# First stage of a fused transformer layer: when the weight pieces for the scales are loaded, when the next heads' weights are split, and when GpSimd clears the stacked operands

## The chip, the core and the metric

The kernel runs on one core of a Trainium2 chip. The metric is the time of one execution on the device in microseconds, as the median of several runs. Lower is better.

## What is computed

The reference is a transformer layer whose attention and MLP branch both read the same layer-normalized input, and whose outputs are added to it (2048 rows, 512 columns, 32 heads of 16, MLP width 1792, all float32):

```
xn = _layernorm(x, axis=-1)
return x + _A_ref(xn, A_wqkv, A_wo) + _B_ref(xn, B_w1, B_b1, B_w2, B_b2)

# _A_ref: scores = einsum("bhqd,bhkd->bhqk", q, k) * (Dh ** -0.5); p = softmax(scores)
#         o = einsum("bhqk,bhkd->bhqd", p, v); return o @ wo
# _B_ref: h = gelu(einsum("bsd,df->bsf", x, w1) + b1); return einsum("bsf,fd->bsd", h, w2) + b2
```

## The kernel before

Matrix products run on TensorE in float16, each operand being split into a high and a low half, so that three products (high by high, high by low, low by high) stand for one. Weights are first divided by a power of two near a bound of their size, the scale, which is found from the sum of the absolute values of each row, one weight piece (128x1024 numbers, 512 KB) at a time. ScalarE reads a piece and gives the sum (`total`, line 937, the only use of the piece at that point); the same weights are read again later, when they are split.

Attention is done in units. A task is one group of four heads by one block of 512 queries; it has 16 units, and there are 32 tasks, 512 units. For each unit TensorE computes scores once for their maxima (`pS`, line 174 by way of `s_mm`), of which VectorE takes the row maxima (line 403), and, 19 units later (LEAD), the same scores with the maximum already subtracted (`pT`), of which ScalarE takes the exponential (line 444, four for each unit), and then the product with V (`pV`). Between these, TensorE works on what is dense (`pD`): projections, and later the MLP and the output projection. The maxima of a task are turned into two rows of the stacked operand `qst` by way of a small store to memory and two loads (lines 358 and 363).

The first stage, up to the first exponential, is written as a list of steps (class `Plan`): each step has an engine, an estimated duration, the steps that it comes after, buffers that it takes and frees, and a weight called tail. The planner repeatedly takes the engine that can start first and emits the step with the largest tail among those that can start. It so fixes the order of instructions on every engine. The engines' queues are worked through in that order on the chip; a step waits there for the data and the buffers that it really needs, not for all that the list names. The first stage normalizes x, turns it (`xt`), projects the first heads' Q and K, stacks them by way of memory (`qk_d`, then `kst` and `qst`, line 549), computes V for the first 12 of 16 tiles (`wvh`, copied into `vv` at line 1187), takes the maxima of 19 units, and meanwhile sums 18 weight pieces (line 1249). A piece takes one of three buffers `wch`; its load is issued by SyncE at line 929. When the estimate of its size reaches BULK (600), the planner holds the load back until the transfers ahead of it are nearly done (line 245).

GpSimd clears the stacked operands `kst` and `qst`, two sets of four blocks (line 95; eight fills for each set), and writes V's column of ones (lines 1136 and 1137). These steps wait for nothing in the list before, and have a low tail.

After the first stage the units run. `rest` yields the remaining dense work: four tiles of V, one projection of the first heads, then the projections of the heads m = 1, 2, 3. The weights of the heads m are loaded by `load_qk` (line 606, on SyncE, as a job in a lane that holds back large transfers) and split by `split_qk`: ScalarE makes the high half (line 154), GpSimd the low one (lines 156 and 157). `split_qk` is stepped once for each unit and yields as long as the pair (m, w) is not in `here`:

```
            while (m, w) not in here:
                yield
            split_pool(wh[:, w, 0], wh[:, w, 1], wf[w], inv[:, 8 + 2 * min(m, 2) + w:9 + 2 * min(m, 2) + w])
```

Of the kernel before, what the change touches and what calls it, by code (L numbers as in the profile page):

```python
# [28 lines left out]
NQB = S // QB  # L29
# [10 lines left out]
NV = 12  # L40
PAIRED = (0, 1), (2, 3), (4, 5), ((0, 1), (0, 2)), (6, 7), (8, 9), (10, 11)
SPLIT, SWITCH, SAME, KLAG = 4, 160, 1500, (0, 0, 12000, 12000)
LAG, E_TAIL = 3000, 8000
LANE = 225
WFROM, WSTEP, XN = 10, 4.5, 4.5
VT = 2600, -8000
# [12 lines left out]
def layer_kernel(ctx: ExitStack, tc: tile.TileContext, x, wqkv, wo, w1, b1, w2, b2, out):  # L59
# [30 lines left out]
    def clear(i, blocks=range(NQB), which=(1, 0)):  # L90
        for b in blocks:
            for st, v in ((qst, 0.0), (kst, MROWS)):
                if (st is kst) not in which:
                    continue
                nc.gpsimd.memset(st[i][b].rearrange("p h n -> p (h n)").bitcast(F32), v)
# [57 lines left out]
    def split_pool(hi, lo, src, inv):  # L153
        nc.scalar.activation(hi, src, AF.Copy, scale=inv)
        given("act", 1000)
        nc.gpsimd.tensor_scalar(src, src, inv, 0.0, op0=ALU.mult, op1=ALU.add)
        nc.gpsimd.tensor_tensor(lo, src, hi, op=ALU.subtract)
# [62 lines left out]
    class Plan:  # L220
# [7 lines left out]
        def add(self, engine, ns, fn, after=(), take=(), free=(), size=0, tail=0, gap=0, small=False, lag=0):  # L228
            t = dict(gap=gap, small=small, lag=lag, e=engine, ns=ns, fn=fn, after=[a for a in after if a], take=take, free=free, size=size, tail=tail,
                     end=None, n=len(self.todo))  # L230
            for key in free:
                self.users.setdefault(key, []).append(t)
            self.todo.append(t)
            return t
# [62 lines left out]
    queue, slot = [], [0]  # L297
# [3 lines left out]
    def later(n, fn, local=False, bulk=0):  # L301
        queue.append((slot[0] + n, fn, local, bulk))
# [292 lines left out]
            if self.key is not None:  # L595
                free_banks[self.key[1]].append(self.key[0])

    here = {(1, 0), (1, 1)}

    def load_qk(m):  # L600
        wf = []
        for w in range(2):
            wf.append(ph.tile([P, D], F32, name="wq", bufs=2).rearrange("p (c n) -> p c n", n=P))

            def load(w=w):
                nc.sync.dma_start(wf[w], wqkv[:, w * D + m * P:w * D + (m + 1) * P].rearrange("(c p) n -> p c n", p=P))
                here.add((m, w))

            later(0, load, True, 256)
        return wf  # L610

    def split_qk(m, wf, inv, ready_w):
        wh = ph.tile([P, 2, 2, NC, P], F16, name="wqk_h", bufs=2)
        for w in (1, 0):
            while (m, w) not in here:
                yield
            split_pool(wh[:, w, 0], wh[:, w, 1], wf[w], inv[:, 8 + 2 * min(m, 2) + w:9 + 2 * min(m, 2) + w])
            yield
        ready_w[m] = wh
        if m < 3:  # L620
            later(4, lambda: wfs.append(load_qk(m + 1)), True)
# [229 lines left out]
    with ExitStack() as st1:  # L851
# [44 lines left out]
        add = plan.add  # L896
# [7 lines left out]
        def raw(key, tag, shape, bufs):  # L904
            tl[key] = (px if tag == "xs" else work if tag == "pe" else ph).tile(shape, F32, name=tag, bufs=bufs)
            return tl[key]
# [19 lines left out]
        def piece_in(key, src, after=(), tail=0):  # L926
            def fn():
                tl[key] = raw(key, "wch", [P, 4 * W], 3).rearrange("p (a b) -> p a b", b=src.shape[2])
                nc.sync.dma_start(tl[key], src)
            return add("SP", 420, fn, after, take=[key], size=520 if tail else 700, tail=tail)  # L930

        def total(ns, key, dst, after, done=()):

            def fn():
                v = tl[key]
                o = v if done else junk[:, :v.shape[1] * v.shape[2]].rearrange("p (a b) -> p a b", b=v.shape[2])
                nc.scalar.activation(o, v, AF.Abs, scale=1.0 / SPREAD, accum_out=dst)
            return add("ACT", ns, fn, after if isinstance(after, list) else [after], free=done)
# [34 lines left out]
        q_in = {w: wq_in(0, w) for w in (1, 0)}  # L973
        wvv = wqkv[:, 2 * D:3 * D].rearrange("(c p) n -> p c n", p=P)
        v_in = [piece_in(("wch", "v", i), wvv[:, :, i * W:(i + 1) * W], tail=280000) for i in range(2)]
        x_in += [tile_in(t) for t in range(4, NT)]

# [134 lines left out]
        s_of, s_prev, m_prev = {}, [None], []  # L1112
# [19 lines left out]
        cleared = {}  # L1132
        his, los, w_ready, k_ready, q_ready, t_last, staged = {}, {}, {}, {}, {}, {}, {}
# [3 lines left out]
            nc.gpsimd.memset(vv[:, :, H * VW:], 0.0)  # L1137

        his[0], los[0] = turned(0, normal(0))
        for b in range(NQB):  # L1140
            for w in (1, 0):
                cleared[w, b] = add("POOL", 480, lambda w=w, b=b: clear(0, [b], [w]), tail=-8000)
        cleared["v"] = add("POOL", 1300, clear_v, tail=-8000)
        q_sum = [total(560, ("wq", 0, w), amq[:, w:w + 1], q_in[w]) for w in (1, 0)]
        chain, inv0, fac0 = scale_chain(amq, 2, q_sum, "q0")
        for w in (1, 0):
            wf, hi, lo, i1 = ("wq", 0, w), wqh[:, w, 0], wqh[:, w, 1], inv0[:, w:w + 1]
            h = add("ACT", 620, lambda wf=wf, hi=hi, i1=i1: nc.scalar.activation(hi, tl[wf], AF.Copy, scale=i1), [chain], free=[wf] if w else [])
            if w:
                w_ready[w] = add("DVE", 700, lambda wf=wf, hi=hi, lo=lo, i1=i1: nc.vector.scalar_tensor_tensor(  # L1150
                    lo, tl[wf], i1, hi, op0=ALU.mult, op1=ALU.subtract), [h], free=[wf])
            else:
                a = add("POOL", 800, lambda wf=wf, i1=i1: nc.gpsimd.tensor_scalar(tl[wf], tl[wf], i1, 0.0, op0=ALU.mult, op1=ALU.add), [h])
                w_ready[w] = add("POOL", 1100, lambda wf=wf, hi=hi, lo=lo: nc.gpsimd.tensor_tensor(lo, tl[wf], hi, op=ALU.subtract), [a], free=[wf])
        a = add("DVE", 90, lambda: nc.vector.tensor_tensor(sexp[:, 0:1], fac0[:, 0:1], fac0[:, 1:2], op=ALU.mult), [chain])
        a = add("DVE", 90, lambda: nc.vector.tensor_scalar_mul(sexp[:, 0:1], sexp[:, 0:1], DH ** -0.5), [a])
        add("ACT", 800, lambda: fetch_scale(0), [a])
# [8 lines left out]
        for i in range(2):  # L1166
            hi, lo = (wvh[j][:, :, i * W:(i + 1) * W] for j in range(2))
            key = ("wch", "v", i)
# [4 lines left out]
            else:  # L1173
                b = add("POOL", 1240, lambda key=key: nc.gpsimd.tensor_scalar(
                    tl[key], tl[key], inv_v[:, 0:1], 0.0, op0=ALU.mult, op1=ALU.add), [h])
# [62 lines left out]
        def low(t):  # L1238
            t["tail"] = -20000
# [6 lines left out]
        for n, src in enumerate(every[:NM]):  # L1246
            key = ("wch", "m", n)
            dst = am_all[:, 12 + n:13 + n] if n < 2 else am_all[:, n - 2:n - 1] if n < 9 else amx[:, n - 2:n - 1]
            low(total(1150, key, dst, piece_in(key, src, k_ready[1]), done=[key]))

        def fill(a, b):
            if b - a > 500 and not s_of:
# [338 lines left out]
```

## Time and profile before

| What | Value |
|---|---|
| Time, median of 3 runs | 1469.04 us (1466.7 to 1472.21) |
| Time of the profiled execution | 1471.15 us |
| Its span, first to last instruction | 1469.4 us |
| TensorE busy | 1440.3 us (98%) |
| VectorE busy | 1348.5 us (92%) |
| ScalarE busy | 1257.0 us (86%) |
| GpSimd busy | 689.4 us (47%) |
| Granted TensorE clock, mean | 0.992 |

The profile is one execution. A row of the order of time gives the start and the duration in us, the engine, the line, the operation, what it writes and reads, how many in a row, and, in brackets, how long the engine was idle ahead of it and what ended that. PE is TensorE, PEld its weight loads, DVE VectorE, ACT ScalarE, POOL GpSimd, SPq the DMA queue that SyncE issues to. A window gives the busy time and the count of each engine in a stretch, the granted TensorE clock as a share of full speed, the busy share of the 16 DMA engines and what they moved in GB/s. "Issue" is time in which an engine waited for nothing that the profile shows.

### The profile page before, as it was taken

The numbers are of one execution on the slowest core, as the hardware profiler recorded it, in microseconds if no ns is written. First come the engines' busy times: TensorE is split into PE (matmuls) and PEld (weight loads), VectorE is DVE, ScalarE is ACT, GpSimd is POOL, SyncE is SP. The second block draws the span as 40 slices with busy tenths as digits, with TensorE's granted clock in tenths as the row PEclk, the third lists the DMA queues.
The fourth block names the chain that finished last, engine by engine and source line by source line (L and its number), as shares of the span: only waits on it lengthen the run. The fifth ranks groups of instructions, "written<-read, shape, count | busy, mean of one in ns | idle before, by whom it ended". The sixth has DMA issues, their size and how long they took to land.

```text
span 1469.4 us, 90770 instructions
## 1 busy us (share of the span) xinstructions
PE 1440.3 (98%) x41229; PEld 974.2 (66%) x41229; DVE 1348.5 (92%) x2236; ACT 1257.0 (86%) x2394; POOL 689.4 (47%) x774
## 2 busy tenths in 40 slices
PE   8979999999999999999999999999999999999998
PEld 4546667766666777766677766666666667666664
DVE  7869799999999999999999999999999999999933
ACT  6548788888999988899988899998889998888885
POOL 5101665755778521268941137783126787212200
PEclk9999999999999999999999999999999999999999
DMA  6550455546323311131112111122102110212413
GB/s 204 179 178 4 152 156 181 164 146 211 107 62 95 100 45 33 38 87 44 52 36 78 42 44 41 44 87 59 38 16 87 58 37 20 59 54 78 118 58 109
DMA packets 111482, 124.98 MB, mean 85 GB/s; under 512 B 21244, under 2 KB 83068, under 8 KB 111096
## 3 DMA queue, kind: packets, MB, share of 16 engines
q1 hardware_dynamic: 111096, 119.18, 26.5%
q8 instruction: 322, 5.28, 1.5%
q14 instruction: 64, 0.52, 0.1%
HBM read 81.66 MB, written 37.34 MB: 81 GB/s over the span
## 4 chain that ended last, share of the span: by engine, by line
PE 90%; DVE 4%; DMA 2%; ACT 1%; issue 1%; SPq 1%; POOL 0%; POOLq 0%; DVEq 0%; ACTq 0%
PE pD L174 27%; PE pV L174 26%; PE pT L174 21%; PE pS L174 16%; DVE mt L403 3%; DMA wq<-in_A_wqkv_dram 1%; PE pT L1049 0%; PE pD L1049 0%; DMA wch<-in_A_wo_dram 0%; ACT pe L444 0%; DMA rb<-den_d 0%; DMA den_d<-dn 0%; DVE wvh L1171 0%; DMA ot_d<-ot 0%; ACT pe L1002 0%
## 5 line engine op out<-in xcount | busy, mean ns | idle before, releaser
L403 DVE TENSOR_REDUCE mt<-pS 128x1 f32<-128x512 f32 x2029 | 1279.6, 684 | 55.6 <-PE pS L174 19.5
L444 ACT ACTIVATE pe<-pT 128x512 f32<-128x512 f32 x2048 | 1109.1, 599 | 150.2 <-PE pT L174 66.6
L174 PE MATMUL pV<-pe,vv 64*32 64x512 f32 x8192 | 1090.4, 592 | 0.3
L174 PE MATMUL pT<-qst,kst 64*32 64x512 f16 x8192 | 707.7, 379 | 7.9 <-ACT pe L444 7.8
L174 PE MATMUL pS<-kst,qst 62*32 62x512 f16 x8116 | 630.8, 379 | 1.9 <-issue 1.8
L174 PEld LDWEIGHTS <-qst 62*32 62x32 f16 x8192 | 312.0, 91 | 184.9 <-issue 36.2
L174 PE MATMUL pD<-xb,wc 64*32 64x512 f16 x5376 | 363.1, 375 | 0.0
L174 PE MATMUL pD<-w_s,g 64*32 64x512 f16 x5376 | 361.5, 375 | 0.0
L174 PEld LDWEIGHTS <-kst 64*32 64x32 f16 x8192 | 279.6, 91 | 106.3 <-issue 35.3
L174 PEld LDWEIGHTS pV<-pe,vv 64*32 64x32 f32 x8192 | 241.8, 106 | 14.0 <-PE pV L174 5.8
L174 PEld LDWEIGHTS <-wc 64*32 64x32 f16 x5376 | 160.4, 91 | 45.0
L174 PEld LDWEIGHTS <-g 64*32 64x32 f16 x5376 | 162.7, 91 | 39.1 <-issue 0.3
L174 PE MATMUL pD<-xt,wqk_h 64*32 64x512 f16 x2400 | 161.9, 379 | 1.4 <-issue 1.4
L371 POOL TENSOR_SCALAR mparts<-mx 128x16 f16<-128x16 f32 x32 | 6.6, 206 | 303.0 <-DVE mx L369 303.0
L1433 POOL TENSOR_TENSOR xa<-xa,yt 128x512 f32<-128x512 f32 x16 | 20.5, 1282 | 166.2 <-ACT yt L1431 166.1
L174 PEld LDWEIGHTS <-wqk_h 64*32 64x32 f16 x2592 | 78.6, 93 | 25.0 <-issue 6.2
L1387 POOL TENSOR_TENSOR t<-t,hh 128x512 f32<-128x512 f32 x56 | 71.9, 1284 | 4.7
L1380 POOL TENSOR_TENSOR t<-t,hh 128x512 f32<-128x512 f32 x56 | 71.8, 1283 | 4.5
L1385 POOL TENSOR_TENSOR t<-hh 128x512 f32<-128x512 f32 x56 | 58.3, 1042 | 21.7 <-ACT hh L1408 19.3
L1382 POOL TENSOR_TENSOR g<-t,g 128x512 f16<-128x512 f32 x56 | 65.3, 1165 | 4.7
L501 POOL TENSOR_TENSOR osb<-osb,rb 128x512 f32<-128x512 f32 x31 | 39.9, 1287 | 49.7 <-ACT pe L444 31.9
L174 PE MATMUL pD<-wo_s,oc 64*32 64x512 f16 x816 | 55.0, 376 | 0.0
(161 smaller groups left out, 968.0 us busy)
## 6 DMA issues: line engine op xcount, KB each, us to landing
wc<-w_d SPq DMA_DIRECT2D x56, 256.0 KB
qk_d<-stg SPq DMA_DIRECT2D x32, 256.0 KB
rb<-den_d SPq DMA_DIRECT2D x124, 64.0 KB
wch<-in_B_w_dram SPq DMA_DIRECT2D x14, 512.0 KB
wch<-in_B_w_dram SPq DMA_DIRECT2D x28, 256.0 KB
w_d<-wsp SPq DMA_DIRECT2D x28, 256.0 KB
kst<-qk_d SPq DMA_DIRECT2D x64, 96.0 KB
qst<-qk_d SPq DMA_DIRECT2D x64, 96.0 KB
```

The lines of the kernel that those rows point to most:

```text
L174: p = nc.tensor.matmul(*args, **kw)
L371: lambda: nc.gpsimd.tensor_scalar(parts[:, :, 0], mx[:, 0], 1.0 / MROW, 0.0, op0=ALU.mult, op1=ALU.add),
L403: nc.vector.reduce_max(mt_of[t][:, n // 2 + n % 2 * 2, qt, kb:kb + 1], s, axis=AX.X)
L444: nc.scalar.activation(pe, st, AF.Exp, scale=scale_of[g // 2])
L501: pooled((1280, lambda: nc.gpsimd.tensor_tensor(osb, osb, rb, op=ALU.mult)), (620, lambda: nc.gpsimd.tensor_scalar(ot[:, 0], osb, 1.0, 0.0 ...
L1380: (1280, lambda: nc.gpsimd.tensor_tensor(t1, t1, hh, op=ALU.mult)),
L1382: (1160, lambda: nc.gpsimd.tensor_tensor(g[:, 1, f, :], t1, g[:, 0, f, :], op=ALU.subtract)),
L1385: pooled((1040, lambda: nc.gpsimd.tensor_tensor(t1, hh, hh, op=ALU.mult)), (620, lambda: nc.gpsimd.tensor_scalar(t1, t1, 1.0, 1.0 / GELU_A ...
L1387: (1280, lambda: nc.gpsimd.tensor_tensor(t1, t1, hh, op=ALU.mult)),
L1433: add = lambda: nc.gpsimd.tensor_tensor(xa, xa, yt, op=ALU.add)
```

## The change

Four edits. The load of piece n in the first stage comes, in the planner's list, after the maximum number 3 n instead of after K's second block is stacked, and its size is estimated at 610 instead of 700 (still above BULK). `here` now holds the unit from which a split may come, four later than the one in which the load was issued. The clears of the first set and V's ones come after K's weights are split (`w_ready[1]`); those of the second set still wait for nothing.

```
-LAG, E_TAIL = 3000, 8000
+LAG, E_TAIL, MSTEP = 3000, 8000, 3.0
...
-    here = {(1, 0), (1, 1)}
+    here = {(1, 0): 0, (1, 1): 0}
...
-                here.add((m, w))
+                here[m, w] = slot[0] + 4
...
-            while (m, w) not in here:
+            while here.get((m, w), 1 << 30) > slot[0]:
                 yield
...
-            return add("SP", 420, fn, after, take=[key], size=520 if tail else 700, tail=tail)
+            return add("SP", 420, fn, after, take=[key], size=520 if tail else 610, tail=tail)
...
-        for b in range(NQB):
-            for w in (1, 0):
-                cleared[w, b] = add("POOL", 480, lambda w=w, b=b: clear(0, [b], [w]), tail=-8000)
-        cleared["v"] = add("POOL", 1300, clear_v, tail=-8000)
...
+        for b in range(NQB):
+            for w in (1, 0):
+                cleared[w, b] = add("POOL", 480, lambda w=w, b=b: clear(0, [b], [w]), [w_ready[1]], tail=-8000)
+        cleared["v"] = add("POOL", 1300, clear_v, [w_ready[1]], tail=-8000)
...
-            low(total(1150, key, dst, piece_in(key, src, k_ready[1]), done=[key]))
+            low(total(1150, key, dst, piece_in(key, src, [m_prev[int(MSTEP * n)]]), done=[key]))
```

What this does to the order of instructions. ScalarE at the end of the first stage, before: L937 is the sum of a piece, L1187 the copy of a tile of V, L382 the copy of the first task's maxima, L444 the exponential.

```order
L382 ACTIVATE mturned<-pS 64x64
L937 ACTIVATE wch,amx<-wch 128x1024 x2
L1187 ACTIVATE vv<-pD 128x32x16
L1187 ACTIVATE vv<-pT 128x32x16
L937 ACTIVATE wch,amx<-wch 128x1024
L1187 ACTIVATE vv<-pT 128x32x16 x2
L937 ACTIVATE wch,amx<-wch 128x1024 x4
L444 ACTIVATE pe<-pT 128x512 x14
```

The same place after the change:

```order
L937 ACTIVATE wch,amx<-wch 128x1024 x2
L382 ACTIVATE mturned<-pS 64x64
L937 ACTIVATE wch,amx<-wch 128x1024 x3
L1187 ACTIVATE vv<-pD 128x32x16
L1187 ACTIVATE vv<-pT 128x32x16 x3
L444 ACTIVATE pe<-pT 128x512 x14
```

The four sums that stood between the last copy of V and the first exponential are gone from there; the last three sums now stand ahead of the last four copies of V.

ScalarE in the units, where the weights of the heads m = 2 are split (L154; L470 and L656 are copies of a finished V product and a finished projection), as a piece of the difference:

```order
 L470 ACTIVATE osb<-pV 128x512
-L444 ACTIVATE pe<-pT 128x512 x2
-L154 ACTIVATE wqk_h<-wq,inv_2910 128x512
-L444 ACTIVATE pe<-pT 128x512 x2
-L656 ACTIVATE pf<-pD 128x512
-L444 ACTIVATE pe<-pT 128x512 x2
-L154 ACTIVATE wqk_h<-wq,inv_2910 128x512
+L444 ACTIVATE pe<-pT 128x512 x4
+L656 ACTIVATE pf<-pD 128x512
 L444 ACTIVATE pe<-pT 128x512 x10
```

The first split stood two exponentials behind the copy L470; it now stands behind fourteen, twelve later, and the second one four behind it as before. The splits of m = 1 and m = 3 are where they were, counted in exponentials, and from the MLP on TensorE's order is the same as before.

SyncE in the first stage, a piece of the difference from the store of the keys' last block on: L929 is the load of a piece, L1106 and L1105 the stores of a projection's halves, L549 the load of a stacked operand.

```order
 L549 DMA kst_1_80<-qk_d 48x2x512 x2
-L929 DMA wch<-in_A_wqkv_dram 128x4x256 x2
-L929 DMA wch<-in_B_w_dram 128x4x256
+L929 DMA wch<-in_B_w_dram 128x4x256 x5
 L1106 DMA qk_d<-stg 128x512
 L1105 DMA qk_d<-stg 128x2x512
 L929 DMA wch<-in_B_w_dram 128x4x256
 L549 DMA kst_3_82<-qk_d 48x2x512 x2
-L929 DMA wch<-in_B_w_dram 128x4x256 x4
-L1106 DMA qk_d<-stg 128x512 x2
```

Two pieces (of A_wqkv) had moved further up, ahead of the rows shown; five instead of one piece of w1 now stand ahead of the store L1106. Further down, all 18 pieces are issued ahead of the store of the first task's maxima (L358), where five of them stood behind it before.

On GpSimd the eight fills of the second set (L95) now come first, then the first step of the normalization, then the split of Q's first weights, and only then the eight fills of the first set and V's ones; before, the first set and the ones came first, and the second set stood between the normalization's first step and the split.

## The prediction

> **What bounds the kernel now.** I read the page first (busy shares, the chain that ended last), then the windows of the exponentials, then the order of time of ScalarE, TensorE and the DMA queue where those windows are thin, and last the granted clock there. The chain of the page says what sets the end:
>
> ```profile
> PE 90%; DVE 4%; DMA 2%; ACT 1%; issue 1%; SPq 1%; POOL 0%; POOLq 0%; DVEq 0%; ACTq 0%
> ```
>
> TensorE carries nine tenths of it. So the time falls only where TensorE stops waiting or its clock is higher, and every stop of TensorE is paid in full, since what follows it is again TensorE's. The exponentials (L444 on ScalarE, 128x512 each) are the best measure of progress, since four belong to each unit of work. The windows of that line alone, 14 us each and then 70 us, give us, busy time, count and granted clock:
>
> ```profile
> 100.00:114.00 14.00, 4.21 (x8) 0.65 0.30 96
> 114.00:128.00 14.00, 9.95 (x19) 0.99 0.02 4
> 142.00:156.00 14.00, 11.31 (x22) 1.00 0.24 69
> 156.00:170.00 14.00, 6.23 (x12) 0.76 0.72 217
> 170.00:184.00 14.00, 11.23 (x21) 1.00 0.37 122
> 310.00:380.00 70.00, 56.94 (x105) 1.00 0.56 172
> ```
>
> In the undisturbed stretch there is one exponential each 70 / 105 = 0.667 us, 21 in 14 us. Two stretches fall short: the one from 100 us, where the first stage hands over to the units, and the one from 156 us. Both also have a lowered clock. These two holes are the subject of the prediction.
>
> The first hole, ScalarE in order of time:
>
> ```profile
> 99.81 1.08 ACT L1187 ACTIVATE vv<-pT 128x512 f32<-128x512 f32 x2 [2.63 <-PE pT L174]
> 100.78 1.06 ACT L937 ACTIVATE wch<-wch 128x1024 f32<-128x1024 f32 x1
> ...
> 103.12 1.06 ACT L937 ACTIVATE wch<-wch 128x1024 f32<-128x1024 f32 x1 [0.16 <-DMA wch<-in_A_wo_dram]
> ...
> 106.00 1.06 ACT L937 ACTIVATE wch<-wch 128x1024 f32<-128x1024 f32 x1 [1.73 <-DMA wch<-in_A_wo_dram]
> 106.96 0.19 ACT L937 ACTIVATION_READ_ACCUMULATOR wch<-wch 128x1 f32 x1
> 107.06 1.06 ACT L444 ACTIVATE pe<-pT 128x512 f32<-128x512 f32 x2
> ```
>
> The last copy of V's values ends at 99.81 + 1.08 = 100.89; then four sums of weight pieces stand on ScalarE, the last of them waiting for its transfer, and the first exponential begins only at 107.06. TensorE has by then filled the banks that the exponentials must empty:
>
> ```profile
> 101.75 0.40 PE L174 MATMUL pS<-kst,qst 62*32 62x512 f16 x4
> 107.69 0.61 PE L174 MATMUL pT<-qst,kst 64*32 64x512 f16 x4 [5.54 <-ACT pe L444]
> ```
>
> The second hole, again ScalarE, then the DMA queue, then TensorE:
>
> ```profile
> 157.27 1.08 ACT L444 ACTIVATE pe<-pT 128x512 f32<-128x512 f32 x2
> 161.74 0.72 ACT L154 ACTIVATE wqk_h<-wq,inv 128x512 f16<-128x512 f32 x1 [3.38 <-DMA wq<-in_A_wqkv_dram]
> 162.36 1.07 ACT L444 ACTIVATE pe<-pT 128x512 f32<-128x512 f32 x2
> ```
>
> ```profile
> 154.39 0.96 SPq L606 DMA_DIRECT2D wq<-in_A_wqkv_dram  x2
> ```
>
> ```profile
> 159.95 0.81 PE L174 MATMUL pD<-xt,wqk_h 64*32 64x512 f16 x9 [0.62 <-issue]
> 162.99 0.61 PE L174 MATMUL pT<-qst,kst 64*32 64x512 f16 x4 [2.24 <-ACT pe L444]
> ```
>
> The split of the next heads' weights (L154) sits on ScalarE in program order as soon as its load was issued; the load took from 154.39 to 161.74, and the exponentials behind the split stood still from 157.27 + 1.08 = 158.35 to 162.36.
>
> **The change, part by part.** Sums are made against the profiled execution: 1471.15 us, of which the span is 1469.4. It stands 2.11 above the median of 1469.04, and I carry the difference over to the median unchanged.
>
> *Pieces of the scales.* The bytes and the 18 sums are the same. By the order, no sum of a piece is left between the last copies of V and the first exponential; the last three stand ahead of the last two pairs of copies. So the first exponential is due when V's copies are done, at 100.9, not at 107.06. With exponentials at 0.667 from 100.9 there would be (128 - 100.9) / 0.667 = 40.6 of them by 128 us; the two windows hold 8 + 19 = 27. The 13.6 that are missing are 9.1 us: 6.2 of later start and about 3 of the lowered clock that follows. The clock, in windows of 2 us (the columns are us, then busy time and count of PE, PEld, DVE, ACT and POOL, then the clock, DMA share and GB/s):
>
> ```profile
> 108.00:110.00 2.00, 2.00 (x32) 0.88 (x29) 0.00 (x0) 1.09 (x3) 0.00 (x0) 0.50 0.00 0
> 112.00:114.00 2.00, 2.00 (x32) 0.85 (x23) 1.29 (x2) 1.08 (x2) 0.00 (x0) 0.50 0.00 0
> ...
> 164.00:166.00 2.00, 2.00 (x44) 1.00 (x32) 1.00 (x2) 1.50 (x3) 1.91 (x3) 0.50 0.81 240
> ...
> 66.00:68.00 2.00, 1.93 (x48) 1.06 (x55) 0.00 (x0) 1.09 (x2) 0.00 (x0) 0.65 0.84 239
> 68.00:70.00 2.00, 2.00 (x48) 1.08 (x40) 1.29 (x2) 0.74 (x2) 0.00 (x0) 0.50 0.11 35
> ...
> 86.00:88.00 2.00, 2.00 (x88) 1.25 (x73) 1.85 (x3) 1.27 (x3) 0.00 (x0) 1.00 0.03 9
> ```
>
> After the gap of 5.54 us the clock was 0.50 from 108 to 114, after that of 2.24 it was 0.50 again. I take 8.5 of the 9.1, since the first unit has to fill its banks whatever stands ahead of it; the ends are 3.8 (a gap of 2 us stays there and still costs the clock, see the rivals) and 9.1. [...] The rows have the halved clock after 2.24 us and for 6 us, and I go by the rows.
>
> *The split four units later.* By the order, the first split of this pair moves behind twelve more exponentials, 12 x 0.667 = 8.0 us: from 158.35 to 166.4, 4.6 after the load's landing at 161.74. The other two splits keep their places among the exponentials. The window from 156 us has 12 exponentials of 21: 9 x 0.667 = 6.0 us. The 0.62 us that TensorE waited for its own instructions is not cured by this, so I take 5.5; the ends are 2.2 (the bare gap, with no clock regained) and 6.0. What waits for the later split is GpSimd's half of it and then the projection of the next heads, which by TensorE's order begins where it began.
>
> *Pieces earlier: what they push.* SyncE's queue now issues eleven pieces ahead of the first store of the queries' last block where it issued eight, and ScalarE, which takes its work in order, has eight sums ahead of V's second pair of copies, not five. Three pieces more are 1.5 MB. What they meet:
>
> ```profile
> 40.00:50.00 10.00, 9.50 (x253) 5.45 (x252) 8.37 (x14) 7.24 (x13) 2.28 (x2) 1.00 0.46 142
> 50.00:60.00 10.00, 10.00 (x288) 6.18 (x294) 8.48 (x15) 5.04 (x10) 2.28 (x2) 1.00 0.72 223
> ```
>
> ```profile
> 62.00:64.00 2.00, 2.00 (x74) 1.31 (x59) 2.00 (x4) 0.61 (x3) 0.00 (x0) 1.00 0.99 296
> ```
>
> ```profile
> 61.18 1.06 ACT L937 ACTIVATE wch<-wch 128x1024 f32<-128x1024 f32 x1 [4.85 <-DMA wch<-in_B_w_dram]
> ```
>
> ```profile
> 66.08 0.39 PE L174 MATMUL pT<-wvh,xt 64*32 64x512 f16 x2 [2.00 <-issue]
> ...
> 80.00 1.25 PE L174 MATMUL pT<-wvh,xt 64*32 64x512 f16 x34 [1.38 <-issue]
> ...
> 85.65 0.39 PE L174 MATMUL pS<-kst,qst 62*32 62x512 f16 x2 [1.78 <-issue]
> ```
>
> From 40 to 60 us the DMA engines are free for 5.4 + 2.8 = 8.2 us; 1.5 MB at the 296 GB/s of the full window from 62 us take 5.3. So the pieces fit, and ScalarE's 4.85 us of idle cover three sums of 1.25 (1.06 and the 0.19 that reads the sum). TensorE's three stops for instructions (2.00, 1.38 and 1.78, and 1.7 for the clock at 66 to 70) fall into bursts of pieces; the spread order may soften them or shift them. I take 0, between -6.9 (all gone) and +6.9 (as many again).
>
> *The clears.* They are the same 16 fills and two for V's ones; the second set now comes first, the first set after the weights of K. VectorE's short steps beside the fills at 10.8 us were long:
>
> ```profile
> 10.84 0.55 DVE L961 TENSOR_SCALAR facq<-sc_c 128x2 int32<-128x2 int32 x1
> 10.91 0.47 DVE L997 TENSOR_TENSOR sd<-sd 128x4 f32<-128x4 f32 x1
> ...
> 23.05 0.16 DVE L997 TENSOR_TENSOR sd<-sd 128x4 f32<-128x4 f32 x1
> ...
> 25.39 0.15 DVE L961 TENSOR_SCALAR facv<-sc_c 128x1 int32<-128x1 int32 x1
> ```
>
> These two differ by 0.40 and 0.31, and they stand on the way to the first weights. The first set's fills, each like this one, now run beside VectorE's work on the first block's projection:
>
> ```profile
> 8.98 0.53 POOL L95 MEMSET qst<- 128x512 f32 x1
> ```
>
> I take -0.5; the ends are -1.1 (both differences and about half as much again) and +2.1 (four fills, each waited for by VectorE with TensorE behind it).
>
> The sum: -8.5 - 5.5 + 0 - 0.5 = -14.5 us. 1471.15 - 14.5 = 1456.65 for an execution like the profiled one, 1469.04 - 14.5 = 1454.5 for the median.
>
> **The rivals.**
> - A short gap stays at the hand-over: whatever is next late there (a bank, the rows of the first maxima) leaves about 2 us idle, and the clock still drops, as after 2.00 us at 66. Then 2 + 3.3 of the 9.1 are not won, the first term is 3.8, the sum -9.8, the time 1459. For it speaks that 2 us were enough; against it, that TensorE had its next products ready before 102. Chance 0.10. [...]
> - The split still waits, because SyncE's queue brings the load later: only the hand-over is won, -9.0, the time 1460. It needs a landing 4.6 us later than now. Chance 0.08.
> - The hand-over is held by a transfer all the same, and only the split is won: -6.0, the time 1463. The order speaks against it. Chance 0.08.
> - A new stop in the middle, of the size of that at 64 us with its clock (2.0 + 1.7), happens twice: +7.4, the time 1462. Chance 0.08.
> - The other side: the pieces choke ScalarE. Its queue is in order, so a sum that waits for a transfer holds the copies which free TensorE's banks. If three of the early sums wait 4.85 us each, as at 61.18, where TensorE has no other work, each costs 4.85 and about 3.3 of clock: +24.5, the sum +10, the time 1479. It decides from the point where the transfers moved forward exceed the 8.2 us of free DMA time; they need 5.3. Chance 0.04.
> - The change does nothing that can be seen, each gain being eaten nearby: 1469. Chance 0.02.
>
> **How the numbers follow.** My forecast has 0.56, and 0.04 is left for more than it (the middle's stops gone as well). About 0.5%, 7.3 us, is what a measurement of this kernel can tell from no change, so faster means below 1461.7. Faster: 0.56 + 0.04 + 0.10 + 0.08 = 0.78; same: 0.08 + 0.08 + 0.02 = 0.18; slower: 0.04. The range reaches down to 1447 (the middle's 6.9 and the rest of the clears' gain) and up to 1463, where the cases with only the split and with new stops end; what lies outside is about 1 in 10.
>
> **What would show it.** Right: in the order of time of ScalarE the first exponential follows a copy of V (L1187) near 100 us; TensorE has no gap over 1 us there and a clock of 1.00 from 102 to 114; L154 has no idle time put down to the load of wq, and the window of 14 us that now holds 12 exponentials holds 20 or more. Wrong: ScalarE's sums of pieces show more idle time for transfers than before, with TensorE idle beside them, or the clock falls at another place in the first 100 us.

## The result, and the profile after

| What | Before | After |
|---|---|---|
| Median, first measurement | 1468.6 us (1466.7 to 1472.21) | 1453.2 us (1451.04 to 1458.97) |
| Ratio with its 95% interval | | 0.9898 [0.9864, 0.9933] |
| Median, second measurement | 1468.53 us (1462.94 to 1473.77) | 1455.07 us (1451.94 to 1458.36) |
| Ratio with its 95% interval | | 0.9911 [0.9889, 0.9933] |
| Profiled execution (first) | 1471.15 us, span 1469.4 | 1458.97 us, span 1457.2 |
| Mean granted clock in it | 0.992 | 0.997 |

The change makes the kernel 13 to 15 us faster; the forecast was 14.5. The first profiled execution of after is the slowest of its four, so a second one (of 1454.95 us) is used beside it where they differ.

The chain of the page, after:

```profile
PE 92%; DVE 4%; issue 1%; DMA 1%; ACT 1%; SPq 0%; DVEq 0%; POOL 0%; ACTq 0%
```

DMA has gone from 2% to 1% and TensorE from 90% to 92%: transfers end fewer waits of the chain. The windows of the exponentials (L444 alone: us, busy time and count, clock, DMA share, GB/s) in the stretches that fell short:

```profile
100.00:114.00 14.00, 6.52 (x12) 1.00 0.13 39
114.00:128.00 14.00, 10.82 (x20) 1.00 0.01 4
...
156.00:170.00 14.00, 10.99 (x21) 1.00 0.76 238
```

The second hole is closed: 21 exponentials where there were 12, at a clock of 1.00 instead of 0.76. The first is only partly closed: 12 where there were 8, though the clock is now 1.00 instead of 0.65. ScalarE in order of time shows why:

```profile
99.70 1.06 ACT L937 ACTIVATE wch<-wch 128x1024 f32<-128x1024 f32 x1 [1.58 <-DMA wch<-in_A_wo_dram]
100.66 0.19 ACT L937 ACTIVATION_READ_ACCUMULATOR wch<-wch 128x1 f32 x1
100.91 0.60 ACT L1187 ACTIVATE vv<-pD 128x512 f32<-128x512 f32 x1
...
104.85 1.08 ACT L1187 ACTIVATE vv<-pT 128x512 f32<-128x512 f32 x2 [2.86 <-PE pT L174]
105.82 3.40 ACT L444 ACTIVATE pe<-pT 128x512 f32<-128x512 f32 x6
```

The first exponential stands right behind a copy of V, as forecast, and no stop of TensorE stands there any more. But V's last copy now ends at 105.9, where it ended at 100.9: the first stage itself was 5 us longer. TensorE's order of time has a large part of the cause (only the rows with a stop are shown):

```profile
63.25 0.39 PE L174 MATMUL pT<-wvh,xt 64*32 64x512 f16 x2 [2.43 <-issue]
...
73.73 0.39 PE L174 MATMUL pT<-wvh,xt 64*32 64x512 f16 x2 [2.89 <-issue]
...
78.83 0.39 PE L174 MATMUL pT<-wvh,xt 64*32 64x512 f16 x2 [1.01 <-issue]
...
89.30 1.48 PE L174 MATMUL pT<-wvh,xt 64*32 64x512 f16 x22 [2.60 <-issue]
```

TensorE stood still for 8.9 us in these four, each put down to "issue" (the list of waits from 40 to 101 us gives 9.5 with a fifth), against 5.83 us in the profile before. I call them stops for instructions; that is a reading of the landings given in the last section. This is the step on the pieces in the middle, for which I had taken 0. Behind the last of the four the clock was 0.73 on average from 90 to 95 us (rows in the last section): a fall of the clock at another place in the first 100 us is one of the signs that the prediction named as wrong. The split (L154) has no idle time ahead of it:

```profile
162.69 0.72 ACT L154 ACTIVATE wqk_h<-wq,inv 128x512 f16<-128x512 f32 x1
```

### The profile page after: what moved, and what is told of

Same layout as the page of the kernel before. It is cut to its first block, busy times and chain, and to the rows that moved or that the text cites. A ratio compares the mean times of both kernels' runs of the same rounds, so it can differ in the third digit from the quotient of the medians.

```text
span 1457.2 us, 90753 instructions
## 1 busy us (share of the span) xinstructions
PE 1433.4 (98%) x41221; PEld 967.7 (66%) x41221; DVE 1348.8 (93%) x2236; ACT 1257.4 (86%) x2394; POOL 687.1 (47%) x774
## 3 DMA queue, kind: packets, MB, share of 16 engines
q8 instruction: 322, 5.28, 1.5%
## 4 chain that ended last, share of the span: by engine, by line
PE 92%; DVE 4%; issue 1%; DMA 1%; ACT 1%; SPq 0%; DVEq 0%; POOL 0%; ACTq 0%
PE pD L174 28%; PE pV L174 26%; PE pT L174 21%; PE pS L174 16%; DVE mt L403 3%; DMA kst<-qk_d 0%; DMA wq<-in_A_wqkv_dram 0%; DVE xt L1032 0%; DMA qk_d<-stg 0%; PE pS L1254 0%; DVE bs L989 0%; ACT xt L1023 0%; DVE wvh L1171 0%; ACT pe L1002 0%; DVE ac L1466 0%
## 5 line engine op out<-in xcount | busy, mean ns | idle before, releaser
L444 ACT ACTIVATE pe<-pT 128x512 f32<-128x512 f32 x2048 | 1109.8, 599 | 142.7 <-PE pT L174 61.4
L174 PEld LDWEIGHTS <-g 64*32 64x32 f16 x5376 | 162.2, 91 | 40.4 <-issue 1.1
```

The costliest lines, as they stand in the source:

```text
L174: p = nc.tensor.matmul(*args, **kw)
L444: nc.scalar.activation(pe, st, AF.Exp, scale=scale_of[g // 2])
```

## The experiments

My theory after the first profile: the hand-over and the split give what was forecast, the clears next to nothing, and what the profile lacks was lost to TensorE's stops for instructions. The main rival: those stops are there in every kernel of this family and vary from one execution to the next, so that the change lost nothing to them; then the sum must be made of the three parts in another way.

**The split alone.** The kernel before, with this edit:

```
-    here = {(1, 0), (1, 1)}
+    here = {(1, 0): 0, (1, 1): 0}
-                here.add((m, w))
+                here[m, w] = slot[0] + 4
-            while (m, w) not in here:
+            while here.get((m, w), 1 << 30) > slot[0]:
```

> The kernel before with the split's four units alone. Theory (a stop of ScalarE on the load of the next heads' weights stops TensorE, and the clock falls with it): 5.5 us less than before, 1463, between 4 and 6.5; the window of 14 us that held 12 exponentials holds 20 or more, no idle time of L154 for the load of wq, clock 1.00 there. Rival (the time of that stop is won elsewhere, because bursts of transfers stop TensorE there anyway): 0 to 2 us less, with TensorE waiting for its own instructions in the same place.

Measured: 1461.4 us (1460.36 to 1465.63) against 1469.53, ratio 0.9951 [0.9937, 0.9966], so 7.2 us (5.0 to 9.3) are won. (What is won is taken here and below from the ratio and its interval; the two medians differ by 8.1 us here, and by up to 1.8 us from what the ratio says further on.) The exponentials in the same windows:

```profile
100.00:114.00 14.00, 4.73 (x10) 0.63 0.25 74
114.00:128.00 14.00, 10.60 (x21) 1.00 0.02 5
156.00:170.00 14.00, 10.40 (x20) 1.00 0.72 224
```

The first hole stays and the second closes: 8 exponentials more in the window from 156 us, 8 x 0.667 = 5.3 us. The theory holds in this stretch. The size of the stop is a matter of the execution, though: in the six profiles of this document whose split is not moved, TensorE stopped there for 1.7 to 2.8 us, the clock was halved behind it in three of them, and from the start of the 40th exponential to that of the 100th they took 42.0 to 46.6 us; the six with the split moved took 40.5 to 42.0. The profile on which the forecast rests, 46.6, is the longest.

**The pieces alone.** The kernel before, with `piece_in` and MSTEP of the change:

```
-            return add("SP", 420, fn, after, take=[key], size=520 if tail else 700, tail=tail)
+            return add("SP", 420, fn, after, take=[key], size=520 if tail else 610, tail=tail)
-            low(total(1150, key, dst, piece_in(key, src, k_ready[1]), done=[key]))
+            low(total(1150, key, dst, piece_in(key, src, [m_prev[int(MSTEP * n)]]), done=[key]))
```

> The kernel before with the pieces' two edits alone (each load after maximum 3 n, size 610). Theory (the hand-over's 5.5 us stop and the halved clock behind it go, but the pieces moved forward bring new stops of TensorE in the middle): 4 to 8.5 us less, about 6; no sum of a piece behind the last copy of V, clock 1.00 after the hand-over, more than the 5.2 us of stops for instructions between 40 and 100 us. Rival (the stop only moves into the middle, and the whole change lives from the split): within 1 us of before.

Measured: 1463.11 us (1459.32 to 1465.13), ratio 0.9948 [0.9934, 0.9962]: 7.6 us (5.6 to 9.7) are won. Here too the first exponential follows V's last copy, at 104.07, and the middle has long stops, as the theory had it (7.8 us for instructions from 40 to 101 us, against 5.8 in before). At the split, TensorE still stops:

```profile
156.35 0.40 PE L174 MATMUL pT<-qst,kst 64*32 64x512 f16 x4 [2.35 <-ACT pe L444]
```

but the clock of the 2 us behind it is 1.00, where the stop of 2.24 us in before was followed by 0.50. Without that I put the split's stop at the bare 2.35 us instead of the 6.0 that the prediction has from its windows, so in such an execution the two parts overlap.

**The clears alone.** The kernel before, with the block of clears of the first set moved behind K's weights as in the change.

> The kernel before with the clears' order alone. Theory (VectorE's short steps are freed of the fills beside them, and the planner moves little else): 0.5 us less, between 1 less and 2 more, so not to be told from before; the steps that took 0.55 and 0.47 us take 0.15. Rival (the planner's new order of the first 40 us carries a good part of the change): 2 us less or more, with the first scores clearly earlier.

Measured: 1464.98 us (1463.24 to 1466.68), ratio 0.9962 [0.9949, 0.9975]: 5.6 us (3.7 to 7.5) are won. My theory missed: I had a tenth of this. The rival is nearer in size, but the sign that it named is not there: the first scores for the maxima do not come earlier (32.01 us, before 30.63). Nor does the profile place the gain in the first stage: V's first copy ends 0.5 us earlier than in before, and the first exponential begins 0.3 us earlier (106.75 against 107.06). Of the 4.5 us between the two spans, 1.9 come at the split, which this edit leaves where it was and where the clock was halved for 3.4 us here and for 6.8 in before; the rest comes later and is not explained.

**TensorE kept busy at the hand-over.** The kernel before, and in the gap at the hand-over 24 products of zeros into a bank that is not read:

```
+                    if (e, a, i) == (0, 1, 3):
+                        warm(24)
```

> The kernel before with 24 idle products of zeros on TensorE (5.2 us of work, an empty bank) put into the stop at the hand-over; nothing else changes, ScalarE's sums stay where they were. Theory (the halved clock behind the stop costs about 3 us by itself): 3 us less than before, 1466, with clock 1.00 from 104 to 116 us and the first exponential still near 107. Rival (the clock of the first units is covered, since they have little to do): no change. [...]

Measured: 1465.92 us (1461.95 to 1472.17), ratio 0.9981 [0.9966, 0.9997]: 2.8 us are won, 0.4 to 5.0. ScalarE's order, and so the late start, is that of before; only the clock changes, from 0.65 to 1.00 in this window:

```profile
100.00:114.00 14.00, 6.74 (x13) 1.00 0.24 76
```

The first exponential begins 6.1 us behind V's last copy (105.39 us), where it was 6.2 in before. From its start to that of the 40th pass 26.3 us, in before 29.2. So the lowered clock was about 3 of the hand-over's 9 us, as the prediction split it. The interval of the time is wide, but does not hold the 0 of the rival; the 2.9 us of the exponentials are the theory's 3, for this one execution.

**The changed kernel once more.** No edit.

> The changed kernel once more, unchanged, as the yardstick for the three runs beside it and as a second profile. Time 1453 us, 1451 to 1456. Theory: the places where TensorE waits for its own instructions in the first stage follow from the order of the program, so they come back near 63, 74 and 89 us and add up to 8 to 10 us between 40 and 101 us (9.5 in the first profile). Rival: they fall by chance in each execution; then their sum lies anywhere between 4 and 10 and at other places, and the 5 us by which the middle of the first stage fell behind in the first profile is no property of the change.

Measured: 1455.07 us. The list of TensorE's waits from 40 to 101 us (waiting line, total us, how often, longest), first in the first profile of after, then in the second:

```profile
PE pT L174 <- issue: 9.5, 5, 2.9
```

```profile
PE pT L174 <- issue: 5.3, 3, 2.6
```

The same kernel has 9.5 us of stops in one execution and 5.3 in the next, about as much as before (5.83). Two of the long ones are near their old places (72.14 and 87.17 us), that at 63 us is gone. On the stops the rival is nearer. But the longer middle of the first stage is still there. It can be measured over the same work: behind a short wait for V's first copy TensorE goes on with the row L1019, and from there to the end of V's last copy it has 1435 products in every kernel of this document. In before, after and the second profile of after that row is

```profile
48.58 1.15 PE L1019 MATMUL pT<-ident,pe 128*128 128x128 f32 x8 [0.49 <-ACT vv L1187]
```

```profile
47.43 1.15 PE L1019 MATMUL pT<-ident,pe 128*128 128x128 f32 x8 [0.48 <-ACT vv L1187]
```

```profile
46.20 1.14 PE L1019 MATMUL pT<-ident,pe 128*128 128x128 f32 x8 [0.49 <-ACT vv L1187]
```

and V's last copy in the second profile of after is

```profile
101.38 1.08 ACT L1187 ACTIVATE vv<-pT 128x512 f32<-128x512 f32 x2 [2.86 <-PE pT L174]
```

So the stretch took 100.89 - 48.58 = 52.3 us in before, 58.5 in the first profile of after and 56.3 in the second. In the pieces alone it took 55.1, and in the four other kernels with the old order of the pieces (the split alone, the clears alone, the products of zeros, the second set's clears) 50.4 to 52.2. The two groups do not overlap: moving the pieces forward costs some 5 us in the middle. Part of it is stops for instructions (5.3 to 9.5 us against 4.3 to 7.0), part is lost clock (1.7 to 3.4 us against 0 to 1.7). How large a single stop is, and where it falls, is a matter of the execution, as the rival had it.

**A quarter of the bytes.** The changed kernel; each of the 18 pieces is loaded only in its first quarter, and ScalarE reads that four times, so that its sums take as long (line numbers behind 936 are two higher):

```
-                nc.sync.dma_start(tl[key], src)
+                nc.sync.dma_start(tl[key] if tail else tl[key][:, :1, :W], src if tail else src[:, :1, :W])
...
+                v = v[:, :1, :W].to_broadcast([P, 4, W]) if key[1] == "m" else v
+                o = junk.rearrange("p (a b) -> p a b", b=W) if key[1] == "m" else o
```

> The changed kernel, but the load of each of the 18 pieces brings only the first quarter of it, and ScalarE reads that quarter four times over, so that its sums take as long as before (the scales are therefore those of a quarter of the weights). TensorE's and VectorE's instructions are the same. Theory: TensorE's stops for instructions in the first stage come from the pieces' transfers, which its instructions have to pass; with a quarter of the bytes the stops between 40 and 101 us fall from some 9 us to under 3, and the time is 5 to 8 us below the changed kernel, 1445 to 1448. Rival: the stops have another source (the count of short products); they stay at 6 to 10 us and the time is within 2 us of the changed kernel.

Measured: 1445.37 us (1444.41 to 1446.55), ratio to before 0.9845 [0.9825, 0.9865], and 9.7 below the changed kernel beside it. Of the waits for instructions from 40 to 101 us this is left:

```profile
PE pT L174 <- issue: 0.2, 1, 0.2
```

The stretch from 40 to 100 us as a whole (busy time and count of PE, PEld, DVE, ACT and POOL, clock, DMA share, GB/s), in the second profile of after and here:

```profile
40.00:100.00 60.00, 52.39 (x1553) 30.17 (x1538) 43.84 (x73) 32.19 (x61) 7.41 (x9) 0.94 0.65 198
```

```profile
40.00:100.00 60.00, 59.00 (x1825) 35.53 (x1801) 53.20 (x91) 40.13 (x76) 7.43 (x9) 1.00 0.31 92
```

TensorE has no less work here: the 1435 products from V's first copy to its last take 45.7 us, where they took 58.5 and 56.3. What is less is the traffic, 92 GB/s instead of 198. So the stops come from the pieces' transfers, and cost 6.6 us of busy time and 0.06 of clock in these 60 us; what the traces have on the way from the one to the other is in the last section. Theory held, with more than it asked (9.7 us where it had 5 to 8).

**The same cut in the kernel before.** The same edit on the other side.

> The kernel before, with the load of each of the 18 pieces cut to its first quarter, which ScalarE reads four times over (the scales are those of a quarter of the weights). It shows what the change is worth when the pieces' transfers stop nobody, as the difference to the changed kernel with the same cut (1445.4 us). Theory: the stops of the middle go here too (5.8 us and some 1.7 of clock), and of the hand-over's gap only the part that waited for a transfer goes (1.7 + 0.2 us); the four sums stay between V's last copy and the first exponential, and the split's stop stays. That gives 1468.5 - 7.5 - 1.9, about 1459, and the change is then worth 14 us: 6.6 at the hand-over, 5.5 to 7 at the split, 1.5 to 2 from the clears. Rival: the transfers stopped TensorE in the changed kernel alone to this extent; then this kernel is within 4 us of before, above 1464, and the change without transfers is worth 20 us, as the sum of its parts was.

Measured: 1459.66 us (1456.46 to 1464.12), ratio to before 0.9944 [0.9921, 0.9967]. This is 14.3 above the changed kernel with the same cut, by the ratios to before 14.5 with some 4.5 either way, where the theory had 14 and the rival 20. The order of time of ScalarE has the four sums back at the hand-over (L939 is the sum, L1189 V's copy):

```profile
91.83 1.08 ACT L1189 ACTIVATE vv<-pT 128x512 f32<-128x512 f32 x2 [1.82 <-PE pT L174]
...
96.73 1.06 ACT L939 ACTIVATE wqk_h<-wch 128x1024 f32<-128x1024 f32 x1 [0.42 <-DMA wch<-in_A_wo_dram]
97.70 0.19 ACT L939 ACTIVATION_READ_ACCUMULATOR wqk_h<-wch 128x1 f32 x1
97.79 2.04 ACT L444 ACTIVATE pe<-pT 128x512 f32<-128x512 f32 x4
```

From 92.91 to 97.79 four sums stand between copy and exponential, and hardly a transfer is waited for: it is the sums' place in the order, not the pieces' bytes, that makes the gap. In the changed kernel with the cut there is none:

```profile
91.02 1.09 ACT L1189 ACTIVATE vv<-pT 128x512 f32<-128x512 f32 x2 [2.67 <-PE pT L174]
91.99 4.63 ACT L444 ACTIVATE pe<-pT 128x512 f32<-128x512 f32 x8
```

The exponentials of the two, first of before with the cut, then of the changed kernel with it:

```profile
80.00:122.00 42.00, 17.20 (x32) 0.92 0.12 33
122.00:240.00 118.00, 91.40 (x168) 0.99 0.45 140
```

```profile
80.00:122.00 42.00, 23.82 (x44) 1.00 0.07 22
122.00:240.00 118.00, 93.42 (x172) 1.00 0.52 160
```

By 122 us the lead is 12 x 0.667 = 8.0 us. Of that 1.8 was there at 46 us (the same stop of 0.48 us for V's first copy ends at 48.23 in the one and 46.44 in the other), before any piece matters, but only 0.8 of it is left when V's last copies end (92.91 and 92.11): the changed order of the pieces costs 1.0 in between even with a quarter of the bytes. The hand-over is then 8.0 - 0.8 = 7.2, where the expectation had 6.6. Between 122 and 240 us come 4 x 0.667 = 2.7 more, the split, which in this execution stopped TensorE for 2.64 us. The spans differ by 12.1, the medians by 14.3.

**Only the second set's clears later.** The kernel before; GpSimd's order alone changes:

```
-            add("POOL", 720, lambda k=k: clear(1, [k]), tail=-9000)
+            add("POOL", 720, lambda k=k: clear(1, [k]), [w_ready[1]], tail=-9000)
```

> The kernel before, but with the clears of the second set after K's weights, those of the first set where they were. Only GpSimd's order changes; the other engines have the order of before word for word. It splits what the clears alone won (about 4.5 us). Theory: the fills that ran beside VectorE's short steps at 9 to 13 us made those slow, and all of the gain comes from there: the steps fall from 0.5 to 0.2 us each, the first products of Q and K come 0.9 us earlier than before in relation to the first sum, and the time is 2.5 to 4.5 us below before. Rival: the gain came from the other order that the planner then writes for TensorE and VectorE between 20 and 45 us; then this kernel is within 1 us of before, or slower by up to 1 where the split of Q's weights passes ahead of fills that the first stacks wait for.

Measured: 1467.15 us (1460.7 to 1471.77), ratio 0.9982 [0.9964, 1.0001]: 2.6 us, 0 to 5.3, which decides little. The rows decide more. VectorE in order of time in this kernel:

```profile
11.50 0.17 DVE L961 TENSOR_SCALAR facq<-sc_c 128x2 int32<-128x2 int32 x1
11.58 0.15 DVE L997 TENSOR_TENSOR sd<-sd 128x4 f32<-128x4 f32 x1
...
11.78 0.98 DVE L1005 TENSOR_SCALAR xs<-xs,mv,sd 128x512 f32<-128x512 f32 x2
...
14.55 0.75 DVE L1150 SCALAR_TENSOR_TENSOR wqk_h<-wq,invq,wqk_h 128x512 f16<-128x512 f32 x1
```

and, of the kernel before, the two rows that the prediction does not show:

```profile
11.50 1.37 DVE L1005 TENSOR_SCALAR xs<-xs,mv,sd 128x512 f32<-128x512 f32 x2
...
14.57 1.59 DVE L1150 SCALAR_TENSOR_TENSOR wqk_h<-wq,invq,wqk_h 128x512 f16<-128x512 f32 x1
```

With no fill beside them the three steps are shorter by 0.38, 0.32 and 0.39, 1.1 us in all. L1150 is shorter by 0.84, but it runs beside the split of Q's weights in both kernels, not beside a fill: here GpSimd's own step became longer instead (L1154, 1.53 us against 1.16). So 1.1 us are due to the fills, 0.8 to which of two engines came first. Of the two together only 0.9 reaches the first scores (29.75 against 30.63 us), as the theory had it, and V's first copy; so they do not explain by themselves the 1.8 us of lead above. The other 3 us that the clears won alone are not in this kernel, whose other engines keep the order of before. Where they come from stays open. Fewer stops in the middle they are not, as far as the one profile of the clears alone shows: it has 7.0 us of them from 40 to 101 us, before 5.8.

**Three sums back at the hand-over.** The changed kernel with another size; TensorE, VectorE and GpSimd keep their orders:

```
-            ... size=520 if tail else 610, tail=tail)
+            ... size=520 if tail else 800, tail=tail)
```

> The changed kernel with the size of a piece at 800 in the planner's list instead of 610. TensorE's, VectorE's and GpSimd's orders stay the same; on ScalarE and SyncE the pieces come later, and three sums stand again between the last copies of V and the first exponential. Theory: what the hand-over won is the time of the sums that stood there; three sums of 1.25 us bring back 3.7 us of later start and a gap of some 3 us on TensorE with a lowered clock behind it, so 4 to 6 us slower than the changed kernel, 1457 to 1459, unless the pieces' later place softens the stops in the middle. Rival: the hand-over's gain came from the transfers being done early and not from the place of the sums; then it is within 1.5 us of the changed kernel.

Measured: 1456.13 us (1449.83 to 1459.78), ratio 0.9926 [0.9904, 0.9948], 1.1 above the changed kernel beside it. The number is the rival's, but not its reason. In order of time the gap is there, on ScalarE and on TensorE (this execution is the fastest of its kernel):

```profile
95.79 1.08 ACT L1187 ACTIVATE vv<-pT 128x512 f32<-128x512 f32 x2 [2.65 <-PE pT L174]
...
99.88 4.36 ACT L444 ACTIVATE pe<-pT 128x512 f32<-128x512 f32 x8
```

```profile
100.52 0.40 PE L174 MATMUL pT<-qst,kst 64*32 64x512 f16 x4 [2.39 <-ACT pe L444]
```

V's copies ended at 96.87 and the exponentials began 3.0 us later, near the forecast 3.7; but the clock stayed at 1.00 throughout. From V's last copy to the 40th exponential it is 29.2 us, where both profiles of after have 26.5: 2.7 us are lost there. The middle, from V's first copy to its last, took 50.7 us instead of 58.5 and 56.3, as with the old order of the pieces. So the later place of the pieces loses at the hand-over what it wins in the middle, which the expectation had left open with its "unless".

**One sum back.** The same edit with 700.

> The changed kernel with the size of a piece at 700 in the planner's list instead of 610: the pieces come a little later, and one sum stands between the last copies of V and the first exponential, where the changed kernel has none and size 800 had three. Tried as a version that may beat both, since a burst of pieces is shorter. Theory: what is lost to one sum at the hand-over (1.25 us) and what is won by fewer stops in the middle are of the same size, so it is within 2 us of the changed kernel (1455), as size 800 was. Rival: a lasting gain of 3 us or more from the shorter bursts, 1452 or less.

Measured: 1454.64 us (1452.45 to 1458.4), ratio 0.9903 [0.9879, 0.9927]: the same as the changed kernel (0.9911). Its profile lies between the two: 54.5 us in the middle and 27.1 from V's last copy to the 40th exponential. No version was found that beats the changed kernel and still reads all weights.

## Why the prediction was right

The total came out (13 to 15 us against 14.5), and its two large terms did; that the sum of all did is luck. The middle, taken at nothing, cost 4 to 6 us, and gains that the forecast did not have made up for it. The stretches of the profiles, in us:

| Stretch | Before | After, first and second profile | Forecast |
|---|---|---|---|
| Start to the row L1019 behind V's first copy | 48.6 | 47.4 and 46.2 | -0.5, the clears |
| From there to the end of V's last copy | 52.3 | 58.5 and 56.3 | 0, the pieces in the middle |
| From there to the start of the 40th exponential | 35.4 | 26.5 and 26.5 | -8.5, the hand-over |
| From there to the start of the 100th | 46.6 | 40.8 and 40.5 | -5.5, the split |
| From there to the end | 1286.5 | 1284.0 and 1283.8 | none |

The last stretch lies between 1281.0 and 1289.0 in the twelve profiles, so that its 2.5 us can be of the execution; they are not explained.

- *What bounds the kernel.* Right. TensorE's stops and its clock are what moved.
- *The hand-over, 8.5.* The mechanism is right: sums on ScalarE between V's last copy and the first exponential. The stretch from V's last copy to the 40th exponential is 8.9 us shorter, to 0.1 us the same in both profiles of after, in the pieces alone and in the quarter of the bytes. Its split into late start and clock is borne out by the products of zeros (2.8 for the clock by the time, 2.9 by the exponentials, 3 forecast), and by the cut in both kernels: 7.2 without most of the transfers' waits. Alone the pieces won 7.6 us (5.6 to 9.7), a balance of this and the middle.
- *The split, 5.5.* Right in mechanism and, within its interval, in size: 7.2 (5.0 to 9.3), though only some 5.3 of the lead in its profile stand in the stretch of the split. The bare gap of 1.7 to 2.8 is sure; the other 3 hang on whether the clock falls, which it did behind 2.24 us in before and did not behind 2.35 in the pieces alone. The forecast is that of an execution in which it falls.
- *Pieces earlier, 0 between -6.9 and +6.9.* This step failed, though inside its ends: the middle became 6.2 and 4.0 us longer in the two profiles of after and 2.8 in the pieces alone. I had compared the bytes with the free time of the DMA engines (5.3 us against 8.2) and concluded that the pieces fit; TensorE's stops I expected to soften or shift, with nothing to show that they would not grow. The stops are made by the pieces' transfers: with a quarter of the bytes the same stretch took 45.7 us in the new order and 44.7 in the old. So the new order costs 1.0 us by itself, and the rest of the loss needs the full transfers. Why they stop TensorE more in the new order, with the same bytes, stays open. Taking them away wins 9.7 us after the change and 8 to 10 before it.
- *The clears, -0.5 between -1.1 and +2.1.* This step was too small. I compared two rows of 0.40 and 0.31 and left out the next step of VectorE behind them, L1005 (0.39), and the meeting of L1150 with GpSimd (0.84), and I costed no effect of the new order. Alone the clears won 5.6 (3.7 to 7.5), outside my ends, but the profiles show 0.5 (the clears alone) to 2.4 (the second of after) by V's first copy, and no cause for the rest. The fear of the other side, fills beside the first block's projection, was unfounded: L1032 took 0.68 us beside them as in before.
- *What is left over.* 7.2 + 7.6 + 5.6 = 20.4 against 13.1 (second measurement). The three half-widths (2.1, 2.1, 1.9) and that of the whole (3.2) leave the difference of 7.3 uncertain by 4.8. Part of it may be the overlap at the split's clock; the rest was not settled. The loss in the middle explains 1 to 3 us of it at most, since the pieces alone have 2.8 us of it too. With the transfers' stops out of the way the whole is 14.3.
- *The rivals.* The short gap that stays at the hand-over did not come in the changed kernel. New stops in the middle, to which I had given 0.08, did come: 2.43 and 2.89 us in one profile, and a longer middle in all three with this order of the pieces, of 2.8 to 6.2 us where the rival had 7.4. That the time still came out as forecast is the luck named above. ScalarE was not choked: its longest wait for a transfer near the hand-over is the 1.58 us shown above.

## What to carry to other kernels

Look for work that nobody waits for yet, but that stands in an engine's queue between the last step of one stage and the first of the next: here its place cost 6.2 us of later start, and 2.8 to 2.9 us of lowered clock behind the gap on top. When a term is "shorter beside less work on a neighbour", add up every step of the chain that ran beside it, not the two that catch the eye. And when a loss in one stretch is in question, measure the same work, from one named instruction to another, in all profiles at hand: here the list of stops of a second profile seemed to clear the change of a loss that every profile with its order of pieces has. A total that comes out does not show that its terms did.

## What the runs showed of the hardware

**The pieces' transfers stopped TensorE.** The page lists a queue named instruction, with packets, MB and share of the engines' time, the same before and after:

```profile
q8 instruction: 322, 5.28, 1.5%
```

These are 5.28 MB / 322 = 16.4 KB each. The queue's packets take 1.5% of the engines' time, and yet TensorE stood still for 4 to 10 us in 60 where pieces of 512 KB kept the engines busy, up to 2.89 us at a time, and for 0.2 us where they were cut to a quarter. The traces' records of single transfers tie the stops to this queue: in the ten profiles with whole pieces there are 46 stops "for issue" of over 0.25 us from 40 to 101 us, and each of them ends 1.2 to 1.6 us behind the landing of one of these packets, of which one lands every 3 to 8 us there. The four of after shown above end at 63.25, 73.73, 78.83 and 89.30 us, the landings ahead of them are at 61.76, 72.19, 77.44 and 88.01. The packets themselves take no longer beside whole pieces (from 40 to 108 us 1.1 us on average in after) than beside quarters (1.1). That TensorE's instructions come in these packets, that a packet starts too late ahead of a stop, and that it stands behind the pieces till then, is my reading and was not shown. What was measured is that with the quarters the traffic from 40 to 100 us fell from 198 to 92 GB/s in the changed kernel and from 192 to 94 in the one before, and that the stops fell with it, from 5.3 to 0.2 us and from 5.8 to none.

**The clock does not follow the length of a gap alone.** It fell to 0.50 behind gaps of 2.24 and 5.54 us in before, and behind 2.64 and 4.25 us in before with the cut; it stayed at 1.00 behind gaps of 2.39 (size 800), 2.35 (pieces alone), 2.43 and 2.89 us (after), and fell again behind 2.60 us in the same profile of after (the window from 90 to 95 us). In the second profile of after it was halved at 51.2 us, behind two waits of only 0.81 and 0.82 us that end at 49.45 and 51.16. The windows behind 2.60 and behind 2.43 us:

```profile
85.00:90.00 5.00, 2.40 (x76) 1.22 (x68) 2.74 (x5) 0.00 (x0) 0.00 (x0) 0.93 0.47 178
90.00:95.00 5.00, 5.00 (x138) 2.40 (x130) 2.46 (x5) 3.16 (x6) 0.58 (x3) 0.73 0.28 93
64.00:66.00 2.00, 2.00 (x88) 1.22 (x79) 1.66 (x3) 0.97 (x2) 0.00 (x0) 1.00 0.37 109
```

In the clock's records the half speed behind gaps of 2.0 to 2.8 us, where it comes, lasts 3.4 us (in before from 66.6 us on, in after from 89.3), in before at the split 6.8 (from 162.2). What decides whether it comes was not shown: gaps of 2.00 and 2.24 us in before were followed by it, one of 2.89 in after was not. In these executions such a gap cost its bare length, and in some of them, as an estimate by half of those 3.4 and 6.8 us, 1.7 to 3.4 us more.
